# Routing attention with an FFN: a new ring of stage loads, DMA issues moved from ACT to SP, and output weights converted later

## The chip, the cores and the metric

One core of a Trainium2 chip runs the whole program. The metric is the device time of one execution in microseconds (us); less is better. The engines are TensorE (PE; PEld is its weight load), VectorE (DVE), ScalarE (ACT), GpSimd (POOL) and SyncE (SP), which here only issues DMAs. Each executes its own instructions in order and waits on semaphores for the others.

## The reference

Attention over 4 batches, 8 heads, 768 tokens and 64 dimensions in which a query sees only the keys of its own cluster (of 16), then a feed-forward block (FFN) with a leaky activation. The FFN's two weight matrices are given as 64-bit floats, all other inputs as 32-bit floats.

```python
q_assign = argmax(einsum('bhsd,hcd->bhsc', q_n, c_n), axis=-1)   # 16 clusters
k_assign = argmax(einsum('bhsd,hcd->bhsc', k_n, c_n), axis=-1)
mask = q_assign[:, :, :, None] == k_assign[:, :, None, :]
scores = where(mask, scale * q @ k.T, -1e9)
attn = softmax(scores) @ v                       # (4, 8, 768, 64)
x = attn.transpose(0, 2, 1, 3).reshape(3072, 512)
h = x @ w_in                                     # 512 x 2048
g = maximum(h, 0) + alpha * minimum(h, 0)
out = g @ w_out                                  # 2048 x 512
```

## The kernel before

The work is cut into 16 pairs: a batch and two heads. Batch 0 (pairs 0 to 3) is done in the *first part*, with all keys against all queries under a mask; a pair takes two halves of three steps, 24 steps in all. The 12 pairs of the other batches are first *ordered*: tokens are sorted by cluster, so that in the *middle part* a chunk of keys meets only the two or three chunks of queries near it. Such a pair takes three steps; its scores all lie in the first of them. The middle part runs from step 24 (`TOGETHER`) to 60. The FFN of batches 0 to 2 is spread over the slots of the middle part, five slots a step less three a pair; that of batch 3, and what was kept back of batch 2, follows behind.

The order of the work is written out by hand: one Python loop over steps and slots appends instructions to the engines. `tick` (L99) begins a slot and issues the next two entries of `loading` on SP; `later` (L94) puts a piece some slots on; `sort_on` (L1222) issues the next entries of the ordering; `convert_next` (L359) begins one weight conversion and `fetch` (L343) issues raw loads for later ones; `feed_down_to` (L1209) issues FFN pieces until the share due by this slot is done. So the code gives the order within each engine, and semaphores give the time.

*Ordering a pair.* `load` brings q and k, `order_features` (L571, DVE transposes), `order_sims` (L576, PE at L582), `order_counts` (an argmax in six DVE pieces, L430 to L437), `order_begins` (L611, PE at L615) and `order_ranks` (L619) give each token its place. Then q, k and v are read into *stage* tiles of 64 + 64 partitions (`order_stage`, L664, three DMAs on SP), and POOL scatters them row by row to a scratch in HBM by indirect DMAs (`order_scatter`, L674, 24 a pair). `order_load` (L688) reads the ordered rows back, and `order_blocks` (L706) transposes them to `qkT` for the scores. There are two stage tiles of a third of a head each (`PARTS = 3`, `STAGES = 2`); a load of the next part stands in the entries of the ordering, half-way through the scatters of the part before. `SIMS` (L1166) says at which step each of the 12 pairs gets its assignment.

*After attention* `normalise_near` (L911) turns a pair's result, `to_rows` transposes it on PE with an ACT copy (L940), `put_back` (L943) sends 12 indirect DMAs from POOL that undo the order, and `fetch_back` (L950) reads the rows back into `x`.

*Weights.* `w_in` and `w_out` arrive as 64-bit floats. `convert` (L240) loads the raw words into a raw tile by a DMA on SP (L244) and makes 32-bit floats in three stages: split (DVE, L250 and L252), scale (ACT, L256 and L258), join (DVE, L262, L265, L268). `w_in` becomes 8 forms of a fast matrix product (`quarters`, L294), of which 7 go to HBM (`sums`). Five raw tiles of 512 columns serve the first part, in which all of `w_in` and the first four row blocks of `w_out` are converted; two tiles of 256 columns serve the middle part, with 24 more pieces of `w_out`.

*FFN.* For each `x` of 8 `hidden` (L1025) makes seven products (L1033) of a form and a sum of x blocks, with ACT copies (L1047 to L1081) and DVE adds and slopes (L1018, L1022) into `gT`; after four of them `final` (L1093) multiplies by `w_out_sb` (L1107). In the first half of the hidden units its result is copied into `y` (L1116), in the second added to it (L1118) and stored. `fetch_sums` (L988) loads two forms into one of four tiles by a DMA that ACT issues (L995), as soon as a tile's last product has been issued; the stores of `y` (L1119) are issued by ACT too.

## Time and profile before

| what | value |
|---|---|
| time, median of 4 runs | 1201.48 us (1190.62 to 1207.32) |
| the profiled execution | 1192.49 us, span 1190.6 us |
| PE busy | 978.0 us (82%), mean granted clock 0.893 |
| DVE, ACT, POOL busy | 526.7, 292.5, 457.0 us |
| first part | to about 188 us |
| FFN without other work at the end | 1028 to 1184 us |

The page gives busy time by engine, the slices of the span with the clock that PE was granted, the chain of work that ended last, and groups of instructions by line; the trace behind it answers for single stretches, engines and lines. A line such as L1033 is one of the program as it was then. "raw<-in_moe_w_out_dram" is a DMA that writes a tile named raw. "remote" and "issue" stand where no recorded event of this core ended a wait. The slices (tenths of busy time in 40 equal parts of the span; PEclk is the granted clock in tenths):

```profile
PE   7898777477596774967887694896999999999997
DVE  6999834456464462536451232432452332430120
ACT  5554422222222230202221130211232220120200
POOL 2016675435657254556746526253403213000000
PEclk8999877689898787988989797796999999999999
```

### The profile page before, as it was taken

Reading aid. Unit: us, or ns where it says so; the run is one execution under the profiler, and the core shown is the slowest. Engines: PE = TensorE matmul, PEld = TensorE weight load, DVE = VectorE, ACT = ScalarE, POOL = GpSimd, SP = SyncE. Lnnn points to the kernel's source line nnn. Section 1 sums busy time; section 2 is a strip of 40 time slices with the busy share of each in tenths; the row PEclk is TensorE's granted clock in tenths of the full one; section 3 lists DMA queues with packets and bytes.
Section 4 is the critical chain, followed back from the end, with each engine's and each line's share of the span. In section 5 each row is a group of like instructions: output and inputs, shape, how many; then the busy total and the mean of one; then the engine's idle time right before and its main releaser. Section 6 shows DMA issues by size and latency. Waiting matters only on the chain.

```text
span 1190.6 us, 12014 instructions
## 1 busy us (share of the span) xinstructions
PE 978.0 (82%) x3931; PEld 482.5 (41%) x3931; DVE 526.7 (44%) x1028; ACT 292.5 (25%) x586; POOL 457.0 (38%) x543
## 2 busy tenths in 40 slices
PE   7898777477596774967887694896999999999997
PEld 4344223243242332433443352442554554454544
DVE  6999834456464462536451232432452332430120
ACT  5554422222222230202221130211232220120200
POOL 2016675435657254556746526253403213000000
PEclk8999877689898787988989797796999999999999
DMA  8888657666464454517653423343351031230211
GB/s 221 229 196 232 182 117 154 157 146 156 116 120 110 104 144 98 121 59 144 158 126 81 97 62 102 88 117 69 102 111 36 26 98 65 68 97 0 73 34 38
DMA packets 344838, 132.63 MB, mean 111 GB/s; under 512 B 295216, under 2 KB 314944, under 8 KB 344768
## 3 DMA queue, kind: packets, MB, share of 16 engines
q1 hardware_dynamic: 311184, 72.59, 30.0%
q10 hardware_dynamic: 19760, 35.57, 10.0%
q0 software_dynamic: 13824, 23.62, 5.9%
q8 instruction: 33, 0.54, 0.2%
q14 instruction: 37, 0.30, 0.1%
HBM read 93.44 MB, written 38.27 MB: 111 GB/s over the span
## 4 chain that ended last, share of the span: by engine, by line
PE 57%; DVE 15%; another core or an unknown queue 11%; issue 9%; DMA 3%; ACT 2%; SPq 2%; POOL 1%; ACTq 0%; DVEq 0%; POOLq 0%
PE fps L1107 24%; PE fps L1033 21%; PE sps L759 2%; PE fps L908 2%; PE mps L908 2%; PE fps L759 2%; DMA form<-sums 1%; DVE power L262 1%; SPq L671 1%; DVE qk L573 1%; DVE forms L309 1%; DMA raw<-in_moe_w_out_dram 1%; PE fps L773 1%; DVE gT L1022 1%
## 5 line engine op out<-in xcount | busy, mean ns | idle before, releaser
L682 POOL DMA_INDIRECT scratch<-stage,off x288 | 290.1, 1007 | 353.5 <-DMA stage<-in_v_dram 153.9
L1033 PE MATMUL fps<-xT,form 128*128 128x384 f32 x896 | 333.4, 530 | 81.8 <-ACT gT L1054 33.5
L1107 PE MATMUL fps<-w_out_sb,gT 128*128 128x512 f32 x752 | 340.3, 608 | 2.6 <-DVE gT L1022 2.6
L1033 PEld LDWEIGHTS fps<-xT,form 128*128 128x128 f32 x896 | 180.2, 207 | 217.4 <-issue 40.1
L1107 PEld LDWEIGHTS fps<-w_out_sb,gT 128*128 128x128 f32 x752 | 144.5, 196 | 175.8 <-issue 170.2
L945 POOL DMA_INDIRECT back<-rows,place x144 | 143.0, 993 | 187.8 <-ACT rows L940 146.6
L1022 DVE SCALAR_TENSOR_TENSOR gT<-gT,alpha 128x768 f32<-128x768 f32 x64 | 64.0, 1015 | 95.7 <-ACT gT L1081 88.7
L1018 DVE TENSOR_TENSOR gT<-gT,fps 128x384 f32<-128x384 f32 x64 | 34.9, 549 | 107.1 <-PE fps L1033 76.0
L759 PE MATMUL sps<-qkT 64*128 64x384 f32 (+1 forms) x240 | 57.1, 546 | 30.1 <-issue 16.0
L1118 DVE TENSOR_TENSOR y<-y,fps 128x512 f32<-128x512 f32 x23 | 15.8, 688 | 118.4 <-PE fps L1107 72.3
L759 PE MATMUL fps<-qkT 64*128 64x384 f32 x240 | 58.5, 551 | 6.1 <-issue 6.1
L1116 ACT COPY y<-fps 128x512 f32<-128x512 f32 x24 | 14.0, 586 | 158.5 <-PE fps L1107 108.0
L786 ACT ACTIVATE E<-sps 128x768 f32<-128x768 f32 (+1 forms) x42 | 31.6, 751 | 81.3 <-PE fps L773 41.4
L783 ACT ACTIVATE E<-fps 128x384 f32<-128x384 f32 x108 | 47.1, 491 | 13.4 <-remote 6.9
L759 PEld LDWEIGHTS sps<-qkT 64*128 64x128 f32 x240 | 20.8, 205 | 61.0 <-issue 36.0
L786 ACT ACTIVATE more<-sps 128x512 f32<-128x512 f32 (+1 forms) x18 | 12.0, 668 | 133.2 <-PE sps L773 80.6
L874 PE MATMUL fps<-E,vt 128*64 128x384 f32 x192 | 41.8, 554 | 2.2 <-issue 1.8
L1047 ACT COPY fps<-fps 128x384 f32<-128x384 f32 x32 | 14.8, 463 | 112.8 <-PE fps L1033 74.6
L256 ACT ACTIVATE power<-power,low_exp 128x256 uint32<-128x256 uint32 (+1 forms) x44 | 26.8, 608 | 56.6 <-DVE power L250 22.7
L867 PE MATMUL fps<-E,ones 128*32 128x192 f32 x384 | 27.2, 373 | 14.7 <-ACT E L786 10.1
L250 DVE TENSOR_SCALAR power<-raw 128x256 uint32<-128x256 uint32 (+1 forms) x44 | 15.9, 362 | 52.7 <-DMA raw<-in_moe_w_out_dram 41.6
L477 ACT COPY aq<-member 32x384 bf16<-32x384 bf16 x62 | 31.5, 508 | 18.2 <-DMA form<-sums 10.9
(187 smaller groups left out, 929.0 us busy)
## 6 DMA issues: line engine op xcount, KB each, us to landing
form<-sums ACTq DMA_DIRECT2D x112, 256.0 KB
qk<-scratch SPq DMA_DIRECT2D x96, 96.0 KB
raw<-in_moe_w_in_dram SPq DMA_DIRECT2D x16, 512.0 KB
sums<-forms SPq DMA_DIRECT2D x28, 256.0 KB
raw<-in_moe_w_out_dram SPq DMA_DIRECT2D x24, 256.0 KB
out_dram<-y ACTq DMA_DIRECT2D x23, 256.0 KB
qk<-in_q_dram SPq DMA_DIRECT2D x48, 96.0 KB
qk<-in_k_dram SPq DMA_DIRECT2D x48, 96.0 KB
```

Source lines behind the costliest of these rows:

```text
L477: nc.scalar.copy(to, members[n][0][r, :])
L682: nc.gpsimd.indirect_dma_start(out=scratch[n][1][h * NX + xx], out_offset=bass.IndirectOffsetOnAxis(ap=ranks[n][:, xx, h:h + 1], axis=0), ...
L759: nc.tensor.matmul(out=bank(ps, h, m), lhsT=qkT[r:r + D, S + c * P:S + (c + 1) * P], rhs=qkT[r:r + D, tokens], start=True, stop=False)
L783: nc.scalar.activation(out=E[:, h, 0:m], in_=ps[h][:, 0:m], func=AF.Exp, scale=SCALE)
L786: nc.scalar.activation(out=E[:, :, 0:m], in_=ps[:, :, 0:m], func=AF.Exp, scale=SCALE)
L874: nc.tensor.matmul(out=po[r:r + D, 0:HS], lhsT=vts[n][:, h, c, :], rhs=e[:, h, :], start=(i == 0), stop=(i == NJ - 1))
L908: nc.tensor.matmul(out=po[r:r + D, to], lhsT=vts[n][:, h, c, :], rhs=E[c][:, h, of], start=c in (1, 4), stop=c == 3)
L945: nc.gpsimd.indirect_dma_start(out=to[i], out_offset=bass.IndirectOffsetOnAxis(ap=place[:, h, j:j + 1], axis=0), in_=rows[:, j, h * D:(h + ...
L1018: nc.vector.tensor_tensor(out=to, in0=to, in1=of, op=ALU.add)
L1022: nc.vector.scalar_tensor_tensor(out=g, in0=g, scalar=alpha[:, f:f + 1], in1=g, op0=ALU.mult, op1=ALU.max)
L1033: nc.tensor.matmul(out=bank(k), lhsT=w[:, cc, :], rhs=rhs[:, cc, :], start=start and cc == 0, stop=cc == KH - 1, skip_group_check=not start)
L1107: nc.tensor.matmul(out=ps[:, 0:DM], lhsT=gs[f][:, half, t * P:(t + 1) * P], rhs=w_out_sb[:, f, :], start=on and f == fs[0], stop=off and f ...
```

## The change

It has six sides that touch one another.

1. The stage tiles hold half a head each (`PARTS = 2`) and there are three (`STAGES = 3`). Loads are no entries of the ordering any more: the parts of all 12 pairs stand in one list, and the scatter `x == 1` of a part asks for the next part not yet loaded; its three DMAs go through `loading`. A scatter is issued only in a slot after its load was issued.
2. `fetch_sums` and the stores of `y` issue their DMAs on SP instead of ACT. A freed form tile is filled one product later than before (`read`).
3. All of `w_out` is converted in the middle part, in 32 pieces of 256 columns. There are nine raw tiles for the first 16 pieces, six of them lent by the pool of `y`, and three for the others; up to four loads may be ahead. The conversions of `w_in` spread over the whole first part.
4. `tick` issues up to three loads. `sort_on` takes 2 and 1 in turn in the first part and 2.33 a slot in the middle, instead of 2 and 3. `order_load` reads `found` last. The second half of the put-backs starts at slot 8 instead of 6.
5. `SIMS` gives the later pairs their assignment later (the fifth at step 26 instead of 22, the last at 47 instead of 44); the FFN of batches 1 and 2 begins one step later.
6. In the middle part there is one `qkT` tile instead of two.

```diff
-    qkp = fast.enter_context(tc.tile_pool(name="qkp", bufs=2))
+    qkp = fast.enter_context(tc.tile_pool(name="qkp", bufs=1))
...
-        for _ in range(min(2, len(loading))):
+        for _ in range(min(3, len(loading))):
             loading.popleft()()
...
-        raw = raw_tiles[0][:, 0:w]
-        raw_tiles.append(raw_tiles.pop(0))
+        raw = raw_of[begun[0] + len(fetched)][0][:, 0:w]
...
-            n = CW if f < FQ else CW // 2
+            n = CW // 2
...
-               and begun[0] + len(fetched) - converted[0] < len(raw_tiles)):
+               and raw_of[begun[0] + len(fetched)][1] < converted[0]):
...
-    PARTS = 3
-    STAGES = 2
+    PARTS = 2
+    STAGES = 3
...
-        raw_tiles[:] = [raw2.tile([P, CW // 2, 2], U32, name=f"raw{5 + i}") for i in range(2)]
-        limit[0], first_ends[0] = W_IN + FQ + 2 * (NF - FQ), now[0]
+        own = [raw2.tile([P, CW // 2, 2], U32, name=f"raw{5 + i}") for i in range(3)]
+        lent = [sorts["ypool"].tile([P, DM], FP32, name="y").bitcast(U32).rearrange(
+            "p (w two) -> p w two", two=2) for i in range(NJ)]
+        both, last_of = lent + own, {}
+        for i in range(2 * NF):
+            j = i % len(both) if i < BORROWED else len(lent) + i % len(own)
+            raw_of[W_IN + i] = both[j], last_of.get(j, -1)
+            last_of[j] = W_IN + i
+        limit[0], first_ends[0] = W_IN + 2 * NF, now[0]
...
-        for i in range(STAGES):
-            sorting.append(lambda i=i: order_stage(n, i))
         for i in range(2 * PARTS):
             for x in range(m):
-                if x == m // 2 and STAGES <= i + STAGES - 1 < 2 * PARTS:
-                    sorting.append(lambda i=i + STAGES - 1: order_stage(n, i))
-                sorting.append(lambda i=i, x=x: order_scatter(n, i, x))
+                sorting.append(((n, i), lambda i=i, x=x: order_scatter(n, i, x)))
...
+    parts_to_come = deque((n, i) for n in range(NO, NP) for i in range(2 * PARTS))
+    staged, loaded_at = {}, {}
+    def order_stage():
+        if not parts_to_come:
+            return
+        n, i = parts_to_come.popleft()
...
         for src, p0, d0 in ((q, 0, 0), (k, TS, 0), (v, TS, D)):
-            nc.sync.dma_start(out=t[p0:p0 + TS, :, d0:d0 + D],
-                              in_=src[b, head, rows].rearrange("(x p) d -> p x d", p=TS))
+            loading.append(lambda src=src, p0=p0, d0=d0: nc.sync.dma_start(
+                out=t[p0:p0 + TS, :, d0:d0 + D],
+                in_=src[b, head, rows].rearrange("(x p) d -> p x d", p=TS)))
+        loading.append(lambda: loaded_at.update({(n, i): now[0]}))
...
+        if x == 1:
+            order_stage()
...
-        starts = (4, 6)
+        starts = (4, 8)
...
-                nc.scalar.dma_start(
+                nc.sync.dma_start(
                     out=t, in_=by_form.rearrange("p x m c w -> p (x m) c w")[:, i:i + AT_ONCE])
...
+                for _ in range(min(1, read[0])):
+                    read[0] -= 1
+                    fetch_sums(1)
                 unused[0] -= 1
-                if not unused[0]:
-                    fetch_sums(1)
+                read[0] += not unused[0]
...
-                stores.append(lambda: nc.scalar.dma_start(out=rows[:, i, :], in_=ys[i]))
+                stores.append(lambda: nc.sync.dma_start(out=rows[:, i, :], in_=ys[i]))
...
-    SIMS = [5, 9, 14, 18, 22] + [26 + SB * i for i in range(2 * NCH - 1)]
+    SIMS = [5, 10, 15, 20] + [26 + SB * i for i in range(2 * NCH)]
...
-    STAGES_OF_FFN = {TOGETHER: (0, SHORT), TOGETHER + PART + SB + 1: (1, SHORT),
-                     TOGETHER + 2 * PART + SB + 1: (2, LONG), NS: None}
+    STAGES_OF_FFN = {TOGETHER: (0, SHORT), TOGETHER + PART + SB + 2: (1, SHORT),
+                     TOGETHER + 2 * PART + SB + 2: (2, LONG), NS: None}
...
-            sort_on(2)
-            if u >= 0 and i == 0 or u in (0, 1) and i == 2:
+            sort_on(2 - i % 2)
+            if (u, i) in ((1, 1), (2, 1)):
+                order_stage()
+            if i == 0 and (0 <= u < 2 * SB or u >= 2 * SB and (u - 2 * SB) % 8 in (0, 2, 3, 5, 6)):
                 convert_next()
...
-            sort_on(3)
-            if i % 2 == 0:
+            sort_on(2 + (at % 3 == 0))
+            if begun[0] < W_IN + BORROWED or at % 2 == 0:
                 convert_next()
-            fetch(2)
+            fetch(4)
```

## The prediction

> **What bounds the kernel now.** I read the stretches first, to find where TensorE (PE) is not the bound, then PE's own timeline for its stops, then the chain of waits behind one stop, then who waits for whom on the other engines.
>
> The stretches (us; busy us and instruction count of PE, PEld, DVE, ACT, POOL; granted clock; DMA share; GB/s):
>
> ```profile
> 0.00:40.00 40.00, 33.20 (x291) 18.59 (x293) 28.08 (x71) 22.28 (x40) 6.60 (x40) 0.91 0.82 228
> 200.00:260.00 60.00, 37.51 (x93) 20.52 (x92) 27.69 (x59) 14.41 (x32) 27.83 (x33) 0.72 0.58 144
> 880.00:1191.00 311.00, 302.96 (x924) 154.82 (x920) 83.28 (x142) 51.06 (x104) 36.08 (x36) 0.99 0.19 55
> ```
>
> From 880 on PE is busy 303 of 311 us at clock 0.99: that stretch is at its bound and the change leaves its matmuls alone. In the first part (to about 188, where the last score of the half-split pairs is over) PE is at 83% and waits little. The loss lies between: in 200:260 PE is idle for 22.5 us and runs at clock 0.72, while no other engine is busy for even half the stretch. So it is waits, not work. PE's timeline there (start, us, what, idle before and its releaser):
>
> ```profile
> 220.89 7.16 PE L1033 MATMUL fps<-xT,form 128*128 128x384 f32 x12 [9.54 <-ACT power L256]
> 234.84 7.01 PE L1033 MATMUL fps<-xT,form 128*128 128x384 f32 x12 [6.79 <-ACT outside L464]
> 248.79 1.01 PE L615 MATMUL mps<-count,row 128*128 128x1 f32 x4 [6.16 <-DVE simT L430]
> ```
>
> The releasers look unrelated, but the chain of waits behind the third stop shows one root:
>
> ```profile
> 238.89 0.66 SPq L671
> ...
> 239.67 4.07 DMA raw<-in_moe_w_out_dram
> ...
> 243.83 0.29 DVE power L250
> ...
> 247.82 0.43 DVE w_out_sb L268
> 248.25 0.50 DVE simT L430
> ...
> 248.79 1.44 PE mps L615 x6
> ```
>
> SyncE (SP) issues three stage loads for the ordering (L671, about 0.6 us each); only then does the raw output weight behind them go out and land; VectorE (DVE) executes in order and stands at L250 until then, with the argmax that PE wants behind it. ScalarE (ACT) stands at L256 behind DVE in the same way. The sums of waits say that this is the rule:
>
> ```profile
> DVE power L250 <- DMA raw<-in_moe_w_out_dram: 41.6, 9, 15.8
> SPq L671 <- DMA scratch<-stage,off: 47.6, 15, 5.9
> SPq L244 <- DVE w_out_sb L265: 22.8, 5, 7.8
> SPq L134 <- DMA form<-sums: 69.3, 13, 16.8
> DVE begin L623 <- remote: 45.0, 3, 20.4
> ```
>
> (us in total, times, longest.) SP waits for the scatters that still read its two stage tiles, and for conversions that still hold its two raw tiles. It also waits for landings of loads that ACT issues: in the built program the DMAs of SP and ACT share eight completion semaphores in turn, so each queue waits for the other's eighth-last DMA. The last line is a second kind of stop: DVE waits up to 20.4 us for a PE result and no recorded event tells why. All three cases fall into long unbroken runs of POOL's indirect DMAs (28 of them at 1.27 us from 427.2 to 464.0, DVE standing from 446.2 to 466.5).
>
> **The change part by part.** All sums are against the profiled execution: 1192.5 us, its span 1190.6, which lies 9.0 us under the median of the four runs, 1201.5.
>
> *Raw tiles, nine instead of two (six lent by y), up to four loads ahead.* The chain above needs a raw load that goes out late; loads that go out several slots before L250 take L250 off it. PE's stops that lead back to L250 or L256 waiting for raw data are 9.54, 6.79, 6.16, and later 5.09 (before 311.25), 6.96 (before 375.00) and 7.92 (before 436.81): 42.5 us. They also cost clock. In 200:260 clock 0.72 means 2 x 0.28 x 60 = 33.6 us at half speed if it has two levels; 22.5 of the 60 us were idle, so at least 11.1 us of work ran at half speed and lost 5.6, at most 16.8: 0.25 to 0.75 us for each idle us. I take 0.37, near the lower end, since the idle time lies mostly inside the slow spells; 42.5 us cost 16 more. What is late next decides how much stays: the scatters, the retrieval, ACT's copies; I keep two thirds: **-28 and -11** (bounds 0 and -74, the latter with 0.75).
>
> The Trainium skill ("TensorE: Matmul & The Clock Gate", HAM oscillation) prices a cold spell at half its throttled time; by that rule the stretch lost 16.8 us to the clock and my term would be -21 in place of -11. This case's rows allow it only as the upper bound, because more than half of the throttled time was idle.
>
> *Output weights out of the first part.* Four 512-wide conversions leave it. On DVE one is 429 + 418 + 679 + 683 + 692 = 2.9 us, so 11.6 us; the fifth pair's assignment leaves too (sims at step 26 instead of 22): two transposes of 0.96, six argmax steps of 0.35 to 0.57, the scan 0.95 and five small ones, about 8 us. PE waited there for DVE only 3.7 + 3.2 + 2.3 us: **-3** (0 to -9). The middle receives eight 256-wide conversions, 0.31 + 0.30 + 0.41 + 0.42 + 0.43 = 1.9 us each, 15 us, and the 8 us. DVE is 46% busy in 200:260, so 32 us of idle time there hide them; without that cover the price is 23.
>
> *Stage loads: four parts a pair, three tiles, issued a part early.* Instead of 18 issues a pair there are 12: 72 fewer in all at 0.6 us, 43 us of SP time. In both kernels a load overwrites the tile of the part before the current one; what is new is that POOL then holds one more part already loaded, so that SP and POOL (153.9 us for stage loads, off the path) no longer stand for each other in turn, and the 47.6 us of L671 waits shrink. One wait on the path is at the seam of the parts: the retrieval of pair 4 went out behind stage loads and PE stood 10.09 us before 183.23. The next late thing is that same retrieval's transpose at 186.8 (L709), so I keep **-3** (0 to -10).
>
> *Form loads and stores from ACT to SP.* ACT loses 112 + 23 issues of 0.33 us, 45 us; SP gains the same, which the 43 us above give back. ACT is 25% busy, so its issue time is not on the path; what counts is that ACT's copies stood behind waiting form issues (2.05 us of idle before L1054 at 389.56, with the issue between): **-2** (0 to -10). Against it: a form load is now behind whatever SP waits for. Queued behind such a wait are forms, stage loads, raw weights, retrievals and stores; who waits is PE at L1033. PE's stock is four tiles of two forms, one of them being read: seven products. 28 products took 36.1 us at full clock (1106.4 to 1142.6), 1.29 us each, so SP may stand 9.0 us before PE notices. SP's rows show longest waits of 11.8 (for returned rows, 11 times, 51.2 us in all) and 16.8: overshoots of 3 and 8 us. **+4** (0 to +60, the upper end in the second rival).
>
> The Trainium skill ("DMA: Bandwidth & Descriptors", Issuing engines are not separate DMA queues) says that issuing from several engines saves the sequencers' issue time and no more; it speaks against this part, since it makes one queue of two and should gain nothing. The L134 row shows what it leaves out: 69.3 us in which one queue stood for the other's landings.
>
> *Put-backs later (second half at 8 instead of 6), scatters 2.33 a slot instead of 3.* POOL's work is the same 432 DMAs. The densest slot held 4 put-backs and 3 entries of the ordering, now 2 and 2.33, and the put-backs spread over six slots instead of five, so the long runs should shorten a little. The stops inside such runs on PE: 9.01 (before 326.83), 7.54 (390.09), 13.54 (467.83), 9.29 (524.32), 8.45 (657.24), 13.47 (746.79), 61 us, with clock 84. Nothing in the trace shows their cause, so the bounds are -84 and +40 (POOL never pausing): **-5**.
>
> *One qkT tile, found last, three loads a tick, FFN stages one step later.* The scores of a pair all lie in its first step and the next pair's transposes in its last, so one tile suffices; found is read only by the put-backs; the later stage start moves FFN work to where PE waits anyway: 0 together. Had the scores not been over by then, every pair would stand for two transposes, 2 us x 12.
>
> Sum: -28 - 11 - 3 - 3 - 2 + 4 - 5 = **-48**: 1144.5 profiled, and with the 9 us between profile and median **1153**.
>
> **The rivals.**
> *Another wait takes the place* (0.13). PE reaches the put-backs and rankings sooner and stands there instead. For: the margin between a pair's last scatter and its retrieval shrinks, since pairs 5 to 11 are assigned three steps later, and DVE already waited 14.6 us at L709 for retrievals. Against: each load still has two steps before its transpose. Of 48 us 42 are lost: 1195. That the loads do not come earlier in time, because SP reaches them no sooner, ends here too.
> *SP as the one queue* (0.17, the other side). Place: the wait for returned rows, once a pair, with the form loads behind it. It decides once SP stands longer than the 9.0 us of stock in every cycle. Price: 5 us a cycle with its clock, 12 cycles, 60, against 31 of the gains kept: +29, 1221 profiled, 1230. For: the 11.8 and 16.8. Against: PE waited only 1.7 us for forms in all although ACT's issues were held up too.
> *The long-run stops go as well* (0.20). If SP's and POOL's backlog is what stretches the runs, half of the 84 us goes on top: 1153 - 42 = 1111.
>
> **How the numbers follow.** My own case, 0.50, reaches from 1128 to 1178 by the halves of its largest terms. A difference under 1% cannot be told from none here (four runs of the kernel spread by 1.4%); 1% is 1189.5 and 1213.5. Faster: 0.50 + 0.20 = 0.70; same 0.13; slower 0.17. The range 1100 to 1210 takes in the first and third case and the wait that takes the place, and leaves out the queue rival and a little of the deep case.
>
> **What would show it.** DVE's wait at L250's counterpart for raw falls from 41.6 to under 10 us, and clock in 200:260 rises above 0.85. PE's wait for form loads stays under 10 us (over 40: the queue rival). SP's waits for ACT's landings vanish. "Remote" waits of DVE's begin stay at tens of us unless the last rival holds. I am wrong if the middle part (188 to 880) is not shorter by 30 us or more, or if the part after 880 changes by more than it moves.

## The result, and the profile after

The change makes the kernel slower: 1219.56 us median (1208.85 to 1233.66, 20 runs) against 1203.72 us (1179.95 to 1216.20, 30 runs), a ratio of 1.025 with a 95% interval of 1.0206 to 1.0294. The profiled execution of the changed kernel took 1226.35 us with a span of 1224.5.

| | before | after |
|---|---|---|
| last product of the first part (E x ones) | 184.3 us | 222.5 us |
| from there to the last product of the FFN | 999.1 us | 996.6 us |
| PE busy, mean clock | 978.0 us, 0.893 | 981.2 us, 0.879 |
| idle spells over 4 us up to 950 us that end with "remote" or "issue": DVE, ACT | 158, 182 us | 246, 341 us |
| longest unbroken run of POOL's indirect DMAs: first part, middle | 12, 28 | 24, 30 |

(A run counts as unbroken where POOL pauses for less than 0.45 us between two instructions.) All of the loss lies in the first part, which the forecast had left nearly alone; behind it next to nothing was gained. These are two single traces. In all that were taken on such chips the first part ends at 184 and 194 us before and at 200 to 222 us after (four traces), and the rest takes 999 and 1004 us before and 987 to 1003 us after. The slices of the changed kernel (tenths of busy time in 40 parts of the span, and the granted clock):

```profile
PE   7974586768849477592949779695999999999998
POOL 2034617340554726464653727274403021100000
PEclk8986777879869789795969979797999999999999
```

PE now has slices of 2, 4 and 5 far into the middle part, and the clock is down to 7 in many of them. The worst place is in the first part. Its stretches (us; busy us and count of PE, PEld, DVE, ACT, POOL; granted clock; DMA share; GB/s), before:

```profile
100.00:160.00 60.00, 51.20 (x384) 21.64 (x382) 43.36 (x91) 23.30 (x43) 38.57 (x45) 0.91 0.73 188
```

and after, with two later ones:

```profile
100.00:160.00 60.00, 32.63 (x198) 12.86 (x198) 25.07 (x55) 8.85 (x16) 33.14 (x39) 0.64 0.59 142
200.00:260.00 60.00, 40.04 (x167) 18.27 (x166) 36.08 (x80) 21.36 (x45) 34.21 (x38) 0.81 0.88 211
910.00:1222.00 312.00, 309.37 (x940) 159.83 (x938) 86.30 (x145) 52.73 (x109) 35.59 (x36) 1.00 0.21 58
```

Between 100 and 160 us every engine does less than before, PE 198 products instead of 384, and the DMA engines are less busy too. So nothing in that stretch became the bound; something held all of them. The tail from 910 on is at its bound, as before. Who waits for whom, after (us in total, times, longest):

```profile
POOL scratch L699 <- issue: 128.4, 271, 16.4
ACT more L806 <- remote: 131.0, 6, 42.5
DVE qk L934 <- remote: 103.2, 7, 27.7
POOL scratch L699 <- DMA stage<-in_v_dram: 16.1, 1, 16.1
PE fps L1053 <- DMA form<-sums: 8.9, 2, 5.2
DVE power L250 <- DMA y<-in_moe_w_out_dram: 2.5, 1, 2.5
```

the row for POOL's loads before,

```profile
POOL scratch L682 <- DMA stage<-in_v_dram: 153.9, 23, 18.8
```

and, after, on SP's queue:

```profile
SPq L1015 <- PE fps L1053: 233.0, 61, 44.7
```

Three readings. POOL waited 153.9 us for stage loads before and now 16.1: the earlier loads do what they are meant to do. DVE's waits for raw output weights (41.6 us before) are down to one of 2.5 us, for a tile lent by `y`. And SP now stands 233 us with a form load for a tile that PE still reads, while PE itself waits for forms only 8.9 us: SP's long wait looks like the queue rival, but nobody waits for it. What grew are the waits that no recorded event ends. One of them, in the timeline of all engines (start, us, what, idle before and its releaser):

```profile
95.14 0.32 PE L793 MATMUL fps<-aq,outside 32*128 32x384 bf16 x1
95.42 0.98 POOL L699 DMA_INDIRECT scratch<-stage,off  x1 [0.28 <-issue]
...
102.08 0.38 DVE L900 STREAM_TRANSPOSE acc<-fps 128x192 f32<-128x192 f32 x1 [11.26 <-remote]
...
102.52 1.50 PE L887 MATMUL fps<-E,ones 128*32 128x192 f32 x13 [7.06 <-issue]
...
107.03 0.13 PEld L887 LDWEIGHTS fps<-E,ones 128*32 128x32 f32 x1 [1.98 <-issue]
...
110.52 0.20 POOL L696 COPY stage<-number 64x6 int32<-64x6 int32 x1
113.39 0.37 SPq L146 DMA_DIRECT2D vt<-in_v_dram  x1
113.39 0.56 DVE L992 TENSOR_TENSOR xT<-fps,acc 128x384 f32<-128x384 f32 x1 [9.10 <-remote]
113.57 0.81 ACT L806 ACTIVATE E<-sps 128x768 f32<-128x768 f32 x1 [18.27 <-remote]
```

POOL issues 24 indirect DMAs from 78.8 to 110.5, one each 1.27 us, without a pause. From 95.5 on, 17 us into that run, all four other engines stand or creep, though the products that ACT and DVE read ended at 95.5 (L793) and 92.1 (L887). Some 3 us after POOL's last DMA all of them go on at the same moment.

### The profile page after: what moved, and what is told of

The parts are those of the page before. It is cut to its first block, busy times and chain, and to the rows that moved or that the text cites. A ratio compares the mean times of both kernels' runs of the same rounds, so it can differ in the third digit from the quotient of the medians.

```text
span 1224.5 us, 11799 instructions
## 1 busy us (share of the span) xinstructions
PE 981.2 (80%) x3931; PEld 479.0 (39%) x3931; DVE 531.7 (43%) x1048; ACT 295.4 (24%) x594; POOL 451.0 (37%) x520
## 4 chain that ended last, share of the span: by engine, by line
PE 59%; another core or an unknown queue 14%; DVE 11%; issue 9%; ACT 2%; SPq 2%; DMA 2%; DVEq 0%; POOL 0%; ACTq 0%; POOLq 0%
PE fps L1129 22%; PE fps L1053 20%; PE sps L779 3%; PE mps L928 3%; PE fps L779 2%; PE fps L894 2%; SPq L135 1%; PE fps L928 1%; PE fps L887 1%; PE sps L793 1%; DVE qk L583 1%; DVE gT L1042 1%; DVE acc L826 1%; PE fps L793 1%
## 5 line engine op out<-in xcount | busy, mean ns | idle before, releaser
L699 POOL DMA_INDIRECT scratch<-stage,off x288 | 286.3, 994 | 230.9 <-issue 128.4
L1053 PE MATMUL fps<-xT,form 128*128 128x384 f32 x896 | 318.0, 511 | 65.7 <-issue 28.6
L1129 PE MATMUL fps<-w_out_sb,gT 128*128 128x512 f32 x752 | 335.9, 602 | 1.2 <-DVE gT L1042 1.2
L1053 PEld LDWEIGHTS fps<-xT,form 128*128 128x128 f32 x896 | 173.8, 199 | 192.6 <-issue 54.7
L928 PE MATMUL mps<-E,vt 128*64 128x256 f32 (+2 forms) x168 | 37.0, 468 | 37.8 <-issue 30.8
L894 PE MATMUL fps<-E,vt 128*64 128x384 f32 x192 | 46.1, 558 | 14.8 <-issue 8.9
L887 PE MATMUL fps<-E,ones 128*32 128x192 f32 x384 | 34.4, 371 | 27.6 <-issue 27.6
L793 PE MATMUL fps<-aq,outside 32*128 32x384 bf16 (+2 forms) x168 | 34.3, 296 | 16.9 <-issue 16.9
L934 DVE TENSOR_TENSOR qk<-fps,acc 128x384 f32<-128x384 f32 x12 | 6.7, 558 | 88.3 <-remote 73.9
L1103 ACT COPY gT<-fps 128x384 f32<-128x384 f32 x32 | 15.3, 479 | 106.7 <-remote 50.7
```

Of the source, the lines that this page charges most:

```text
L699: nc.gpsimd.indirect_dma_start(out=scratch[n][1][h * NX + xx], out_offset=bass.IndirectOffsetOnAxis(ap=ranks[n][:, xx, h:h + 1], axis=0), ...
L793: nc.tensor.matmul(out=bank(ps, h, m)[:, to], lhsT=members[n][1][r, h, i * P:(i + 1) * P], rhs=aqs[n, x][r, a - x * HS:z - x * HS], start= ...
L887: nc.tensor.matmul(out=first_den[r:r + Q, 0:HS // 2], lhsT=ones[:, 0:Q], rhs=e[:, h, x * HS // 2:(x + 1) * HS // 2], start=(i == 0), stop= ...
L894: nc.tensor.matmul(out=po[r:r + D, 0:HS], lhsT=vts[n][:, h, c, :], rhs=e[:, h, :], start=(i == 0), stop=(i == NJ - 1))
L928: nc.tensor.matmul(out=po[r:r + D, to], lhsT=vts[n][:, h, c, :], rhs=E[c][:, h, of], start=c in (1, 4), stop=c == 3)
L1053: nc.tensor.matmul(out=bank(k), lhsT=w[:, cc, :], rhs=rhs[:, cc, :], start=start and cc == 0, stop=cc == KH - 1, skip_group_check=not start)
```

## The experiments

Two theories at first. *L*: a long unbroken run of POOL's indirect DMAs holds up all other engines, and the change lengthens the runs, because POOL's waits for stage loads had broken them. *Q*: SP as the one queue is the cause (the second rival of the forecast).

### The cost by itself, and three edits of the changed kernel

*micro* computes nothing of the reference. A chain of links (product on PE, copy on DVE, copy on ACT, each waiting for the one before) runs beside POOL:

```python
def chain(link):
    a = ps.tile([P, P], FP32, name="fps")
    nc.tensor.matmul(out=a, lhsT=ident, rhs=link, start=True, stop=True)
    b = ring.tile([P, P], FP32, name="half")
    nc.vector.tensor_copy(out=b, in_=a)
    c = ring.tile([P, P], FP32, name="link")
    nc.scalar.copy(c, b)
    return c
```

> This kernel computes nothing of the reference: it writes zeros to the output and measures the disputed cost by itself. A chain of links (matmul, VectorE copy, ScalarE copy, each waiting for the one before) runs beside nine loads of POOL, one after the other: nothing; 8, 16, 32 and 48 unbroken indirect DMAs; 32 with a wait for VectorE after every 8; 32 with a POOL memset after every 8; 32 plain DMAs issued by POOL; 48 memsets without any DMA. Theory L (an unbroken run of POOL's indirect DMAs holds up the semaphores and the issue of all other engines from some 13 us into it until 2 to 3 us after its end, as the traces before and after show around 95.5 to 113.4 us): a link keeps its length of about 1 us beside 0 and 8 DMAs and beside the memsets, stands for 3 to 15 us in the second half of 32 and for longer in 48, and keeps its length where POOL waits after every 8. Theory Q (the stops come from SP, which holds form loads, stage loads and stores in one queue): all links keep the same length within 20%, since SP does nothing here.

Measured: a link takes 1.51 us beside nothing, beside 8 and 16 indirect DMAs (one link of 1.86 apart), beside 4 x 8 of them with waits of 8 to 10 us between, beside 32 plain DMAs of POOL and beside 48 memsets. PE's timeline beside 32 unbroken indirect DMAs, which run from 160.6 to 201.2 us (idle before each product in brackets):

```profile
183.78 0.79 PE L42 MATMUL fps<-link,ident 128*128 128x128 f32 x2 [0.71 <-ACT link L46]
185.28 0.79 PE L42 MATMUL fps<-link,ident 128*128 128x128 f32 x2 [0.71 <-ACT link L46]
189.20 0.79 PE L42 MATMUL fps<-link,ident 128*128 128x128 f32 x2 [3.12 <-ACT link L46]
194.09 0.79 PE L42 MATMUL fps<-link,ident 128*128 128x128 f32 x2 [4.09 <-issue]
198.99 0.79 PE L42 MATMUL fps<-link,ident 128*128 128x128 f32 x2 [4.11 <-issue]
```

From 24.7 us into the run a link takes 3.9 and then 4.9 us, three times as long; the last slow link begins 2.7 us after POOL's end. Beside 48 it slows at the same 24.7 us and reaches 5.6 us; with a memset of POOL after every 8 of the 32 it does both as well. So the onset is later than the 13 us that L had expected. SP does nothing here, so Q cannot make these stops, and L holds for the mechanism.

*a_pace* ties POOL to the slots by a word that DVE writes:

```diff
+    def pace():
+        mark = marks.tile([1, 2], FP32, name="mark")
+        nc.vector.memset(mark[:, 0:1], 0.0)
+        nc.gpsimd.tensor_copy(out=mark[:, 1:2], in_=mark[:, 0:1])
...
     def sort_on(m):
+        if sorting:
+            pace()
```

> The changed kernel, with one mark a slot: VectorE writes one word in each slot that may issue entries of the ordering, and POOL reads it before it goes on, so that POOL cannot run ahead of the slots and its indirect DMAs come in runs of 2 to 6 instead of 24 to 30. Theory L: the waits of DVE and ACT that no recorded event ends (remote and issue over 4 us: 258 and 341 us in the changed kernel) fall below 80 us each, the clock rises in all stretches between 40 and 860, and the time falls by 80 to 130 us, to 1090 to 1140. Theory Q: the scatters come later, so that the retrievals do too, and the time stays at 1220 or rises to 1235.

Measured: 1170.92 us (1165.13 to 1173.96), some 49 us less than the changed kernel's 1220; the kernel before spread from 1179 to 1215 us beside it, with one execution at 1681. The first part ends at 193.2 instead of 222.5. The size of L's forecast was missed, and its trace says why: POOL still has runs of 20 to 36 in the middle part, since it catches up once a late mark comes, and the spells remain at 163 us on DVE and 233 on ACT. Behind the first part it gains too (964.3 us instead of 996.6), although its runs there are no shorter; L does not explain that. Q's forecast fails.

*a_ring2* has two stage tiles, lets a part's scatters start in the slot of its load, asks for the next load one scatter earlier and takes one entry more a slot in the middle part:

```diff
-    STAGES = 3
+    STAGES = 2
...
-        if x == 1:
+        if x == 0:
...
-            if sorting and loaded_at.get(sorting[0][0], now[0]) < now[0]:
+            if sorting and loaded_at.get(sorting[0][0], 1 << 20) <= now[0]:
...
-            if (u, i) in ((1, 1), (2, 1)):
+            if (u, i) == (1, 1):
...
-            sort_on(2 + (at % 3 == 0))
+            sort_on(3 + (at % 3 == 0))
```

> The changed kernel with two stage tiles instead of three, still of half a head, and a part's scatters allowed in the slot in which its load was issued: a load then goes out only one part ahead, into the tile whose scatters have just been issued, and POOL waits for it after every six DMAs. Theory L: the runs fall to 6 to 12 DMAs, the waits that no recorded event ends halve, and the time falls by 40 to 90 us, to 1130 to 1180. Theory Q: SP now waits for scatters in front of form loads as well, so the time rises by 10 to 40 us.

Measured: 1220.86 us (1214.99 to 1227.26), as the changed kernel: neither forecast holds. The first part, with runs of 6 to 18, ends at 204.1, which is within what the changed kernel's own traces show. In the middle part the runs stay at 15 to 36, and SP now waits more for scatters (33.2 us in the changed kernel):

```profile
SPq L685 <- DMA scratch<-stage,off: 76.5, 22, 10.6
```

POOL waits for stage loads again, 158.4 us in 13 waits of up to 33.3, about as long in sum as the kernel before (153.9 in 23). But they are fewer and longer and leave the runs between them as they were, and the time stays too. So the sum of these waits is not what counts; how often they break the runs may be. The edit did not shorten the runs as it was made to, and says no more.

*a_act* gives form loads and stores back to ACT:

```diff
-                nc.sync.dma_start(
+                nc.scalar.dma_start(
                     out=t, in_=by_form.rearrange("p x m c w -> p (x m) c w")[:, i:i + AT_ONCE])
...
-                for _ in range(min(1, read[0])):
-                    read[0] -= 1
-                    fetch_sums(1)
                 unused[0] -= 1
-                read[0] += not unused[0]
+                if not unused[0]:
+                    fetch_sums(1)
...
-                stores.append(lambda: nc.sync.dma_start(out=rows[:, i, :], in_=ys[i]))
+                stores.append(lambda: nc.scalar.dma_start(out=rows[:, i, :], in_=ys[i]))
```

> The changed kernel with form loads and the stores of y issued by ACT again, each form load as soon as a tile's last product has been issued, as before. Theory L: the runs of POOL stay, so the time stays within 12 us of the changed kernel (1208 to 1232). Theory Q: SP no longer stands for PE at form loads (233 us of waits in the changed kernel), and the time falls by 30 us or more, below 1190.

Measured: 1219.17 us (1211.12 to 1231.35). The 233 us of SP's waits for PE are gone and the time is the same, as L expected: Q is out.

### Runs of eight at most

Next came a stop inside POOL alone. After every eighth indirect DMA it writes a word that this DMA reads, and so stands until it has landed:

```diff
+    sent, RUN = [0], 8
+
+    def breathe(word):
+        sent[0] += 1
+        if sent[0] % RUN == 0:
+            nc.gpsimd.memset(word, 0.0)
...
             in_=t[:, x, :], in_offset=None,
             element_offset=h * 2 * S * P)
+        breathe(t[0:1, x, 0:1])
...
             in_=rows[:, j, h * D:(h + 1) * D], in_offset=None, element_offset=h * S * D)
+        breathe(rows[0:1, j, h * D:h * D + 1])
```

> The changed kernel; after every eighth indirect DMA POOL writes one word of the source that this DMA reads, a word that is not needed any more, so that it stands until the DMA has read it. No other engine is involved, and the order of the work is the same. Theory L: no run is longer than eight, so the waits of DVE and ACT that no recorded event ends fall below 60 us each, the first part ends by 190 us instead of 222, and the time falls to 1110 to 1165. Rival S (pacing helped because the scatters came later or in step with the slots, not because the runs were broken): the time stays within 15 us of the changed kernel's 1220.

> The kernel before with the same stop after every eighth indirect DMA. Theory L: its runs of 14 to 28 cost 61 us of stops of PE and some 20 of clock, so the time falls by 30 to 75 us, to 1130 to 1175; the other sides of the change show in what the changed kernel with the stop is faster than this one: 25 us or more if the raw tiles and the other sides gain what was predicted for them (48), within 10 if they gain nothing. Rival S: within 15 us of 1204.

*b_ring3* goes the other way, and gives the kernel before its loads earlier:

```diff
-    qkp = fast.enter_context(tc.tile_pool(name="qkp", bufs=2))
+    qkp = fast.enter_context(tc.tile_pool(name="qkp", bufs=1))
...
+    qkp_first = first_part.enter_context(tc.tile_pool(name="qkp1", bufs=2))
...
-            qkTs[n] = qkp.tile([P, NB * P], FP32, name="qkT")
+            qkTs[n] = qkp_first.tile([P, NB * P], FP32, name="qkT")
...
-    STAGES = 2
+    STAGES = 3
...
             nc.gpsimd.memset(stage[0], 0.0)
+            nc.gpsimd.memset(stage[2], 0.0)
```

> The kernel before with a third stage tile of a third of a head, and one qkT tile in the middle part to make room for it: a load is asked for one part earlier, so that POOL waits for fewer of them. Nothing else of the change. Theory L: the runs grow to 16 to 24, those of the first part above all, the first part ends 10 to 35 us later than 184, and the time rises by 8 to 35 us, to 1212 to 1240. Rival (earlier loads are harmless, and the loss of the changed kernel comes from another side of it): 1185 to 1205.

*micro2* varies the run of 48 DMAs:

> Computes nothing of the reference, as the first measurement of this kind: the same chain of links, 1.51 us each when undisturbed, beside 48 indirect DMAs of POOL in six ways: with a POOL write after every 4, 8 or 16 that must wait until the last of them has landed; with a POOL copy after every 8 that waits for a VectorE write made long before, so without a stop; unbroken with 64 rows instead of 128; unbroken with rows of 256 bytes; and last beside 96 plain DMAs issued by POOL. Theory B (POOL writes more per indirect DMA than can be drained meanwhile, a backlog fills after some 25 us, and a pause of 1 to 2 us lets it drain): links stay at 1.51 us with a stop after every 4 and 8, and slow down late or slightly with every 16; the copy that need not wait changes nothing, so links slow to 4 or 5 us from about 25 us on; 64 rows shift the onset or remove it; short rows change nothing, since the number of rows is the same; plain DMAs do nothing. Theory I (POOL's instruction stream itself, unbroken by any semaphore, shuts out others): the copy that need not wait removes the slow links as well.

All four went to another chip, and there everything was different: the kernel before took 1074.99 us (1072.72 to 1085.63, 13 runs) instead of 1204. *b_ring3* took 1031.78, a ratio of 0.9577 (0.9501 to 0.9653); *a_own8* 1086.02, 1.009 (1.0058 to 1.0122); *b_own8* 1122.56, 1.0431 (1.0367 to 1.0495). No link of *micro2* was slow, not even beside 48 unbroken DMAs, and in none of the three traces does DVE, ACT or PE have a single spell over 4 us that ends with "remote" or "issue", although *b_ring3* has runs of 36 and 40. So all four expectations missed on that chip, for one reason: it does not do what L describes. Call it a chip of the second kind. What the stops cost where they cure nothing can be read there: 48 us in the kernel before.

That made a sharper theory, *L2*: long runs disturb on chips of the first kind only; where they do not, or where they are broken, the change gains. Its rival *C*: the second chip is only quicker in general.

### Both kinds of chip

So the kernels were measured again on chips of either kind.

> The changed kernel with POOL's stop after every eighth indirect DMA again, 1086 beside 1075 for the kernel before on a chip without the long stops. Theory L2: with no run over eight there is nothing left that differs between the chips, so it takes 1075 to 1110 on either: beside about 1204 for the kernel before it is 8 to 10% faster, beside 1075 the same as then. Rival C: beside 1204 it takes 1170 or more, like the kernel that was paced by slots.

> The changed kernel itself again, beside the kernel before on the same chip. On the chip of the second batch the kernel before takes 1075 us instead of 1204, and no trace from it has a wait that no recorded event ends, although POOL's runs there reach 40 DMAs. Theory L2 (the long runs hold up the other engines on some chips and not on others): if the kernel before takes about 1075 here, the changed kernel takes 1015 to 1050, faster by 2 to 6%, since then only the gains of its earlier loads are left (the third stage tile alone gave 43); if it takes about 1204, the changed kernel takes 1209 to 1234 again. Rival C (that chip is only quicker in general, and the change loses there too): 1085 to 1110 beside 1075.

Both on a chip of the first kind, beside 1202.39: the changed kernel 1220.61 (ratio 1.0178, 1.0098 to 1.0258), with the stops 1099.79 (0.915, 0.9071 to 0.9228). With 432 / 8 = 54 short stops of POOL 121 us are gone; the time comes within 14 us of the same kernel's on the second kind. Two stretches of the kernel with the stops, columns as above:

```profile
100.00:160.00 60.00, 48.52 (x334) 20.75 (x336) 38.01 (x82) 21.72 (x41) 35.55 (x44) 0.86 0.70 162
400.00:550.00 150.00, 125.35 (x482) 61.49 (x480) 83.31 (x151) 34.78 (x73) 98.65 (x118) 0.90 0.57 130
```

What most of its stops (those behind scatters) cost POOL, from its waits (total, times, longest):

```profile
POOL stage L87 <- DMA scratch<-stage,off: 75.0, 31, 4.4
```

And the later stretch of the changed kernel without them:

```profile
400.00:550.00 150.00, 101.24 (x386) 49.05 (x384) 69.33 (x137) 32.19 (x69) 78.57 (x85) 0.85 0.50 113
```

PE runs 482 product instructions in these 150 us instead of 386, and POOL, though it pays 2.4 us for a stop (75.0 over 31), gets through more too: 118 instructions, the stops among them, instead of 85. Some spells remain (42 us on DVE, 145 on ACT), where the same kernel on the second kind has none, and its first part ends at 185.2 instead of 171.9.

> The kernel before with the third stage tile again: 1032 beside 1075 on the chip without the long stops. Theory L2, where the kernel before takes about 1204: the same edit lengthens POOL's runs and so costs what it gained, 1190 to 1240, with over 200 us of waits that no recorded event ends on DVE and on ACT; where it takes about 1075: 1032 again. Rival (the third tile is a gain on every chip, and the loss of the changed kernel has another root): 1150 to 1175 beside 1204.

Measured on the first kind: 1203.50 beside 1202.62, ratio 1.0086 (1.0036 to 1.0136). The edit that gains 43 us on the second kind gains nothing here, with 161 us of spells on DVE (over 200 had been expected) and 234 on ACT, with runs of up to 32, and its first part ends at 199.6 instead of 178.3.

> The chain of links beside six ways of issuing 48 indirect DMAs again; in the first run of it no link was slow in any of them, the unbroken ones included, on the chip where the kernel before takes 1075. Where it takes about 1204, theory B (a backlog that a pause of 1 to 2 us lets drain): links of 1.51 us with a stop after every 4 and 8, slow ones late or few with every 16, slow ones from 25 us on with the copy that need not wait, a later onset or none with 64 rows. Theory I (an unbroken instruction stream): the copy that need not wait removes them too.

Measured on the first kind; stretches of the trace, one for each way of issuing (the first count is PE's, two records for each link):

```profile
120.00:191.00 71.00, 37.26 (x94) 23.49 (x94) 13.78 (x49) 13.99 (x47) 46.63 (x54) 1.00 0.13 45
214.00:282.00 68.00, 34.62 (x88) 21.95 (x88) 12.92 (x47) 13.10 (x44) 46.46 (x52) 1.00 0.14 47
309.00:370.00 61.00, 18.96 (x48) 12.00 (x48) 6.69 (x23) 6.84 (x23) 46.98 (x54) 1.00 0.15 51
430.00:488.00 58.00, 16.70 (x42) 10.51 (x42) 5.99 (x22) 5.95 (x20) 43.02 (x49) 1.00 0.12 27
```

and the third of them in *micro2*, on the second kind:

```profile
305.00:367.00 62.00, 32.40 (x82) 20.48 (x82) 12.19 (x44) 12.21 (x41) 47.40 (x55) 1.00 0.15 50
```

The rows are: a stop after every 8 (47 links, none slow), after every 16 (44 links, two slow ones at the very end), a copy after every 8 that need not wait (24 links, slow from 24.7 us on) and 64 rows unbroken (21 links, slow from 20.2 us on). Rows of 256 bytes behave like the third, a stop after every 4 like the first, and 96 plain DMAs disturb nothing. So a real pause is what helps, and 1.7 us of it after every 8 is enough (DMAs then stand 3.0 us apart instead of 1.27); a semaphore without a wait does not, so theory I falls. Halving the rows, or their bytes, does not remove it, and against B's forecast 64 rows do not put it off either: so its onset is not set by the rows or the bytes. It begins with the 17th to 20th DMA of a run, 20.2 to 24.7 us into it; which of the two counts, the number or the time, is not told apart. The slow links at the end of the runs of 16 show that it also builds up over several runs with short pauses.

> The changed kernel with POOL's stop after every twelfth indirect DMA instead of every eighth: a third fewer stops of 2 to 3 us each, and runs of 15 us. By the measurement with links a run of 16 is too short to disturb them, while in the whole kernel before the stops began 13 to 20 us into a run. Theory B: beside 1204 for the kernel before 1075 to 1110, about as with eight; beside 1075 for it 1060 to 1085, a little less than with eight (1086).

Measured on the first kind: 1103.27 (1096.43 to 1109.53), ratio 0.9277 (0.9174 to 0.9381): as good as with eight, within what can be told. Yet its spells are 115 us on DVE and 155 on ACT, not far from the kernel before (158 and 182), and its first part ends at 196.7. So runs of 12 with pauses of some 2 us are not free of them, and the sum of the spells is no measure of the time.

> The kernel before with POOL's stop after every eighth indirect DMA, 1123 beside 1075 on the chip without the long stops. Theory L2: beside 1204 it takes 1120 to 1145, 20 to 45 us more than the changed kernel with the same stop (1100), which is what all other sides of the change are worth once the runs are broken in both. Rival (the change loses also apart from the runs): 1100 or less.

Measured on the first kind: 1134.45 (1128.43 to 1139.77) beside 1196.55, ratio 0.9455 (0.9354 to 0.9555). Its spells are 70 us on DVE and 121 on ACT. With broken runs the change is worth 1134 - 1100 = 35 us there, and 1123 - 1086 = 37 us on the second kind.

> The changed kernel again, for the chip on which the kernel before takes 1075. Theory L2: there it takes 1015 to 1050. Rival C: 1085 to 1110 there. Where the kernel before takes 1204, it takes 1209 to 1234 by both.

> The changed kernel once more; so far it ran only on chips where the kernel before takes 1204. Theory L2: beside 1075 for the kernel before it takes 1015 to 1050; rival C: 1085 to 1110. Beside 1204 it takes 1209 to 1234 by both, and nothing is learnt.

Both fell to the first kind and repeat the result: 1220.52 (ratio 1.0263, 1.0127 to 1.04) and 1214.86 (1.0136, 1.0038 to 1.0233).

> The changed kernel once more, for a chip of the kind on which the kernel before takes 1075 us: there theory L2 expects 1015 to 1050, rival C 1085 to 1110. Beside 1204 nothing new: 1209 to 1234.

Measured on the second kind: 1023.27 us (two runs) beside 1075.56, ratio 0.9515 (0.9487 to 0.9542). L2 holds and C falls: where the runs disturb nobody, the very same program is 52 us faster than the one before. The stops after every eighth cost it 63 us there (1086 beside 1023). Its slices and two stretches:

```profile
PE   7997875587798779899699999999999999999997
POOL 3007677460477777777777777730404021000000
PEclk8998977797899889999799999999999999999999
```

```profile
100.00:160.00 60.00, 49.82 (x420) 21.11 (x412) 43.57 (x97) 24.34 (x46) 43.28 (x48) 0.91 0.74 179
400.00:550.00 150.00, 135.32 (x544) 66.18 (x540) 87.00 (x149) 36.75 (x74) 115.87 (x123) 0.95 0.66 147
```

POOL is at 7 tenths or so without a break (its longest run is 72 DMAs), and PE at 9 from the middle on.

> The kernel before, for its trace on a chip of the second kind, where it takes 1075 us. Theory L2: there its runs of 14 to 28 DMAs are in the trace as on the first kind, but DVE and ACT have no wait over 4 us that no recorded event ends (158 and 182 us on the first kind), and the stops of PE that lead back to late raw output weights and the seam stop of some 10 us are still there. POOL's waits for stage loads (153.9 us on the first kind) show what the third stage tile took away. On a chip of the first kind it repeats the trace of before, 1180 to 1216.

Measured: 1206.84, a chip of the first kind again. It repeats the first trace (150 us of spells on DVE, 183 on ACT, the first part to 194.1), and a trace of the kernel before on the second kind is missing.

## Why the prediction was wrong

One term was wrong in sign and size. The others were about right in their sum, but not in their shares. The terms without the one for long runs came to -43. Measured without disturbance they are -52 (second kind), and -35 to -37 with the stops on either kind. On the second kind the kernel goes from 1075 to 1023, a gain of 52 where the sum said 48. That this comes so near is in part luck: the third stage tile, counted with -3, gives -43 there by itself, without the new raw tiles, which were counted with -39. On the chips where the kernel before takes 1204 the long runs decide, and they put the time outside the forecast's range.

**The failed step is "Put-backs later, scatters 2.33 a slot": "the long runs should shorten a little ... -5".** It judged the runs by the number of DMAs in a slot. They depend on what makes POOL wait, and the same forecast says a few paragraphs earlier that POOL's 153.9 us of waits for stage loads shrink; it called them "off the path" and dropped them. They were among the pauses that broke the runs. In the first part of the kernel before, runs of 4 to 12 have pauses of 0.5 to 4.8 us between them, and PE's stops stay at some 3 us until the seam. Four of the nine pauses, the two longest among them, end with a stage load:

```profile
106.04 0.98 POOL L682 DMA_INDIRECT scratch<-stage,off  x1 [4.81 <-DMA stage<-in_v_dram]
113.63 0.98 POOL L682 DMA_INDIRECT scratch<-stage,off  x1 [2.21 <-DMA stage<-in_v_dram]
145.68 1.04 POOL L682 DMA_INDIRECT scratch<-stage,off  x1 [1.74 <-DMA stage<-in_v_dram]
185.20 0.98 POOL L682 DMA_INDIRECT scratch<-stage,off  x1 [4.74 <-DMA stage<-in_v_dram]
```

After, three runs of 24 stand there, and the part takes 38 us longer in these traces. That the earlier loads alone cost as much as they gain there is what *b_ring3* shows: -43 us on the second kind, none on the first. Behind the first part the gains of the change and the longer runs cancel (999.1 and 996.6 us). Comparing the kinds gives the price: 1203.7 - 1075.0 = 128.7 us in the kernel before and 1219.6 - 1023.3 = 196.3 in the changed one, so the term comes out, as this difference, at +68 in place of -5. It lies outside the bounds that were given too (-84 and +40), and even "the stops inside such runs", 61 us with 84 for the clock, were too small a count: by the same comparison it is 129.

Such a difference contains whatever else may differ between the chips. That it is the runs is shown by the stops: they bring the changed kernel from 1220 to 1100 on the first kind, beside 1086 on the second, and the kernel before from 1197 to 1134, beside 1123.

Point by point, for the rest:

- *Raw tiles (-39).* The wait fell as forecast (41.6 us to 2.5). The clock's part was misread: in 200:260 of the kernel before the trace has 33.8 us of clock at 0.5, and PE is busy in 20.6 of them, not 11.1. So 39% of that time was idle and not more than half, and the loss is 10.3 us, 0.46 for each idle us where 0.37 was taken. The worth of the part alone was not shown: on the second kind *b_ring3*, which leaves the raw tiles as they were, still has such waits, and is only 9 us slower than the whole change. From its waits there:

```profile
DVE power L251 <- DMA raw<-in_moe_w_out_dram: 42.6, 12, 11.1
POOL scratch L683 <- DMA stage<-in_v_dram: 37.0, 14, 10.3
```

- *Stage loads (-3).* Mis-sized: the third tile alone gives -43 on the second kind. So the sum came out right there with its parts wrongly shared; since either part may remove the same stops, the shares stay open, as does the way by which the third tile gains so much. The second line of the fence shows only that POOL waits 37.0 us for loads there; the 153.9 of the kernel before are from the other kind of chip.
- *ACT relieved (-2), SP as one queue (+4).* Their sum is near nothing: on the first kind *a_act* undoes both and takes 1219 for 1220. SP's waits for form tiles were expected as waits that others would feel; they are 233 us and PE waits for forms 8.9, inside the "under 10" of the forecast (13.7 on the second kind).
- *Weights out of the first part (-3).* Not told apart; the first part of the changed kernel ends at 167.4 us where it is not disturbed, and at 171.9 against 191.7 with the stops in both kernels (second kind), so it gained more than 3; how much of it is due to the stage loads is open.
- *What would show it.* Right: raw waits, form waits, SP's waits for ACT's landings, which are gone. Wrong: the clock in 200:260 (0.81, not above 0.85), what follows the first part (2.5 us shorter, not 30), and the "remote" waits of DVE's begin: it has none any more, and such waits grew at other lines.

The rival "the long-run stops go as well" had the right object and the wrong sign; the one on the losing side of the forecast named SP's queue, which *a_act* excludes. No rival said that runs could grow; only the bound of +40, "POOL never pausing", allowed for it. The change's list of parts held it: whoever removes a wait of an engine whose long runs are known to hurt must count what that engine does with the time.

The Trainium skill ("SBUF — State Buffer", Who interferes with whom), where it tells how the engines share their access to SBUF, allows one contention only, between DVE and GpSimd at a shared pair of ports, and says that PE and ACT never wait on anyone. In the trace above ACT stands 18.27 us and PE 7.06 with no event recorded that either waits for. The measurement decides: that rule does not cover these stops.

## What to carry to other kernels

A wait that looks free can be a pause that something else needs. Before removing it, ask what the engine will do without it, and look for places in the profile where long unbroken work of that engine goes with idle time that no event explains. Where POOL issues many indirect DMAs, break their runs at 8 to 12 by letting POOL wait for its own last one: here 1220 us became 1100 (and the kernel before 1197 became 1134) on the chips that mind, for 48 us lost in the kernel before and 63 in the changed one on a chip that does not. And time a change on more than one chip before believing either sign: this one is 2.5% slower on one kind and 4.9% faster on another.

## What the runs showed of the hardware

- On two of three chips unbroken indirect DMAs of POOL, one each 1.27 us, slow a chain of PE, DVE and ACT from the 17th to the 20th on (20.2 to 24.7 us): its three hops take up to 5.6 us instead of 1.51, and the last slow link begins up to 7.3 us after the run. In the whole kernel SP stands as well, and it begins 17 us into the run shown above.
- For the chain a pause of 1.7 us after every 8 prevents it; memsets between do not; plain DMAs of POOL (96, one each 0.53 us) do not cause it. In the whole kernels with such pauses part of the spells stays (42 and 145 us on DVE and ACT after every 8, 115 and 155 after every 12).
- What fills up was not found. A backlog that grows by the DMA rather than by its rows, and that pauses drain, would fit, but is argued, not shown.
- It is a property of the chip, or of its state: of three chips that were told apart, two had it in all traces (medians of the kernel before 1197 to 1208 us) and one in none (1075 and 1076).
